# A state-space and linear-attention kernel on one core: a table factor from three products, parameter rows of 1 KB, two more table loads, and another order of the steps

## The chip, the core and the metric

The kernel runs on one core of a Trainium2 chip. The metric is the time of one execution on the device in microseconds (us). The profile shows five engines: PE (TensorE matmuls, with PEld for its weight loads), DVE (VectorE), ACT (ScalarE), POOL (GpSimd) and SP (SyncE, which issues most of the DMAs).

## The reference, cut to what matters

Both branches read the same input `x = A_u` (2048 positions, 512 channels, bf16).

```python
# branch a: S4 convolution, per channel d with N = 128 complex states
dt = exp(log_dt)[:, None];  A = A_re + 1j*A_im;  logdA = dt*A;  dB = dt*(B_re + 1j*B_im)
P = exp(logdA[:, :, None] * l)                   # l = 0 .. 2047
K = einsum("dn,dnl,dn->dl", C_re + 1j*C_im, P, dB).real
a = causal_conv(x, K) + x * Dskip                # by FFT of length 4096
# branch b: linear attention, 32 heads of 16, features softmax(+-q w_phi), softmax(+-k w_phi)
qkv = x @ wqkv;  kv = phi_k^T v;  z = sum phi_k
b = ((phi_q kv) / (phi_q z + 1e-6)) @ wo
g = sigmoid((x * gate_w).sum(-1));  out = g*a + (1-g)*b
```

The convolution kernel `K` needs the exponential of 512 x 128 complex numbers at 2048 places. The kernel builds it from factors: a place is split into a coarse step (4 values), a middle step (8 values of 64 places) and a fine step, so that a matmul over the 128 states multiplies a left table `A` (coarse times middle, with the coefficients C and dB in it) by a right table `R` (fine).

## The kernel before, in words

**Steps and order.** The program is a list of steps made by `P.add` and `P.dma` (class `Plan`), numbered as the code adds them. `Plan.ORDER` is a string with two base-64 digits for each step: it is the order in which the steps are issued, and so the order on each engine's queue. `SIDES` gives, for each step that ACT or DVE could do (most are evictions of PSUM, by `Plan.copy`, lines 175 and 177), the engine. `FOURS` has a digit for each of the 16 units of 32 channels.

**Parameters** (`prepare`). SP loads the six parameter arrays as 128 partitions by 4 pieces of 128 values (line 242, rows of 256 B), the input as `UD` in 16 DMAs with rows of 256 B (line 1465), the weights `wqk`, and constants. PE turns the parameters (line 334). From them ACT and DVE form the polar tables: `Dtab` (the middle step; magnitudes `p_d` by Exp on ACT, cosines and sines `p_sn` by Sin on ACT, the products `p_dd` and `p_de` on DVE), `Ctab` (the coarse step with coefficients; `p_ce`, `p_fc`, `p_ab`, `p_sn`, then `p_pr`, `p_px`, `p_cn` on DVE) and `Gtab`. Line 347 is the line of nearly all these products. ACT needs a table load (line 93) to go from Exp and Ln to Sin and back.

**Keys** (`keys_and_spectrum`, `attention_keys`). Once the whole input is there, PE turns it (`xT`, line 263), takes the forward FFT of the input (`psAu` to `XAu`, `psBu` to `XU`, written to DRAM as `XUd`), and for 16 blocks of 128 positions makes keys (`pk`), their exponentials on ACT (`ek`), sums on DVE (`zk`, line 662), Ln and Exp (`rz`), values (`vp`, `vb`, `vr`) and the sum `kv` (`kn`). `kvbd` closes this stage.

**Units** (`plan_conv`, `kgen`). For each of 16 units U of 32 channels: PE makes arguments, ACT takes `cs` (two Sin, in four phases of four units, each between two table loads) and `E` (Exp); DVE makes `El` (line 989), `Rh` and `Rl` (the right table, lines 1054 and 1058) and the left table in steps `A1` (line 1037), `A2` (line 1042) and, where the digit of `FOURS` is 0, `A3` (line 1047). `kps` on PE (`kgen_chunk`, line 209) multiplies left by right: 64 matmuls where `A3` has added the products up, 128 where the digit is 1 and PE adds them in PSUM. The left table has one buffer. Then `KD`, FFT stage `psA` to `XA`, `psB` to `XK`, on DVE the product `t` with the input's spectrum (line 1230), `psz` to `Zr`, a way through DRAM (`Zd`, `ZT`), `psy`, and `ou` on DVE with the gate. Beside the units the queries of four blocks run (`pq`, `eq`, `zs`, `z1` to `z5`, `em`, `ops`, `oT`). The last group, units 14 and 15, ends with `zt`, `psy32`, `ou` and the `out` DMAs (line 1341).

```python
terms = [(k, k) for k in range(2)] if not four else [(0, 0), (2, 0), (1, 1), (3, 1)]
...
c.A = g.wk.tile([128, 4, 4, 8, 32], BF16, name="A", tag="A", bufs=g.P.k["A"])   # A1 fills 0:2, A2 fills 2:4
nc.vector.tensor_tensor(out=c.A[:, 0:2], in0=c.A[:, 0:2], in1=c.A[:, 2:4], op=ALU.add)   # A3
```

## Time and profile before

| what | value |
|---|---|
| three runs | 253.78, 251.02, 252.83 us; median 252.83 us |
| the profiled execution | 252.17 us, of which the profile's span is 250.4 us |
| granted TensorE clock, mean | 0.944 |
| busy share of the span | DVE 90%, ACT 84%, PE 81%, PEld 57%, POOL 1% |
| DMA | 38.23 MB in 61922 packets, mean 153 GB/s |
| chain that ended last | PE 28%, DVE 24%, ACT 23%, DMA 10%, SP's queue 7%, issue 5% |

How to read it: busy time of an engine is the union of its instructions. DVE and ACT instructions that follow one another overlap by about 0.1 us, so a stage's time is nearer to the distance of their starts than to the sum of their durations. [...] Idle time of an engine costs only where that engine sets the pace.

### The profile page before, as it was taken

What the parts mean: (1) busy time and instruction counts of PE and PEld (TensorE: products, weight loads), DVE (VectorE), ACT (ScalarE), POOL (GpSimd) and SP (SyncE); (2) the same over time, 40 slices, a digit from 0 to 9 for tenths busy, and PEclk for the clock granted to TensorE, in tenths of its full rate; (3) what the DMA queues carried; (4) which work ended last, traced back from release to release, by engine and by line L of the source; (5) the groups of instructions that cost most, each with busy time, mean ns of one, the idle gap of its engine ahead of it and who ended that gap; (6) DMA issues with size and microseconds to landing.
All of it is one profiled execution on the core that took longest, in us unless ns stands there. A gap on an engine that the chain in (4) does not pass through costs nothing.

```text
span 250.4 us, 9850 instructions
## 1 busy us (share of the span) xinstructions
PE 202.3 (81%) x4412; PEld 141.8 (57%) x4437; DVE 224.2 (90%) x287; ACT 211.0 (84%) x291; POOL 2.4 (1%) x7
## 2 busy tenths in 40 slices
PE   0695999999956468798797778889999789998970
PEld 0584755447734434256456646765777576877550
DVE  0388999989899988999999999999999999999680
ACT  2058999999999999999999999999999999974430
POOL 0200000000000000000000000000000000000000
PEclk9999999999995569999979999999999999999985
DMA  6999910236280477400619129804896879998664
GB/s 134 275 174 159 404 49 4 90 105 134 56 256 0 145 235 223 160 3 13 174 49 240 38 73 243 265 3 92 197 209 192 219 206 234 225 235 165 185 171 75
DMA packets 61922, 38.23 MB, mean 153 GB/s; under 512 B 40632, under 2 KB 57272, under 8 KB 61496
## 3 DMA queue, kind: packets, MB, share of 16 engines
q1 hardware_dynamic: 61880, 37.61, 60.0%
q8 instruction: 34, 0.56, 1.0%
q14 instruction: 8, 0.07, 0.1%
HBM read 24.49 MB, written 13.11 MB: 150 GB/s over the span
## 4 chain that ended last, share of the span: by engine, by line
PE 28%; DVE 24%; ACT 23%; DMA 10%; SPq 7%; issue 5%; ACTq 0%; DVEq 0%
ACT Eq L96 4%; PE pk L635 4%; ACT cs L96 4%; DMA UD<-in_A_u_dram 4%; PE vp L683 4%; SPq L1465 3%; ACT E L96 3%; PE kps L209 2%; DMA ZT<-Zd 2%; PE psB L542 2%; ACT XA L175 2%; ACT L93 2%; DVE t L1230 2%; PE psy L750 2%; PE psz L1256 2%
## 5 line engine op out<-in xcount | busy, mean ns | idle before, releaser
L209 PEld LDWEIGHTS <-A 128*32 128x32 bf16 x1664 | 28.5, 160 | 6.2 <-issue 3.6
L209 PE MATMUL kps<-R,A 128*32 128x64 bf16 x1664 | 30.3, 229 | 1.8 <-DVE A L1042 0.5
L96 ACT ACTIVATE cs<-args 128x1024 bf16<-128x1024 f32 x32 | 30.7, 1050 | 0.2 <-PE args L953 0.2
L1058 DVE TENSOR_TENSOR R<-E,cs 128x2048 bf16<-128x2048 bf16 x16 | 19.5, 1217 | 0.0
L1037 DVE TENSOR_TENSOR A<-Ctab,Dtab 128x2048 bf16<-128x2048 bf16 x16 | 19.5, 1217 | 0.0
L1054 DVE TENSOR_TENSOR R<-E,cs 128x2048 bf16<-128x2048 bf16 x16 | 19.5, 1217 | 0.0
L1042 DVE TENSOR_TENSOR A<-Ctab,Dtab 128x2048 bf16<-128x2048 bf16 x16 | 19.5, 1217 | 0.0
L175 ACT CAST Zr<-psz 128x1024 bf16<-128x1024 f32 (+1 forms) x17 | 16.5, 974 | 2.5 <-issue 1.2
L542 PE MATMUL psB<-XAu,TB 64*128 64x128 bf16 x256 | 12.8, 262 | 7.1 <-ACT xst L175 4.9
L175 ACT CAST XK<-psB 128x1024 bf16<-128x1024 f32 (+1 forms) x15 | 15.0, 1010 | 3.8 <-PE psB L222 2.3
L175 ACT CAST XA<-psA 128x1024 bf16<-128x1024 f32 (+1 forms) x16 | 15.6, 1002 | 3.2 <-PE psA L216 3.2
L683 PE MATMUL vp<-WW,xT 128*128 128x512 bf16 x59 | 16.9, 403 | 0.8 <-issue 0.7
L1230 DVE TENSOR_TENSOR t<-XUX,XK 128x2048 bf16<-128x2048 bf16 x14 | 17.0, 1218 | 0.5 <-ACT XK L175 0.5
L96 ACT ACTIVATE Ek<-pk 128x512 bf16<-128x512 f32 x32 | 16.8, 602 | 0.4 <-PE pk L635 0.2
L769 PE MATMUL pq<-xT,Wqp 128*128 128x512 bf16 x64 | 16.5, 396 | 0.6 <-ACT Eq L96 0.6
L96 ACT ACTIVATE Eq<-pq 128x512 bf16<-128x512 f32 (+1 forms) x28 | 16.7, 711 | 0.2 <-PE pq L769 0.2
L96 ACT ACTIVATE E<-args 128x1024 bf16<-128x1024 f32 x16 | 16.8, 1058 | 0.0
L542 PEld LDWEIGHTS <-TB 64*128 64x128 bf16 x256 | 10.3, 116 | 11.2 <-issue 11.0
L1256 PE MATMUL psz<-t,small 128*128 128x512 bf16 x49 | 14.6, 380 | 2.0 <-ACT cs L96 0.5
L635 PE MATMUL pk<-WW,xT 128*128 128x512 bf16 x57 | 15.5, 380 | 0.5 <-issue 0.2
L662 DVE TENSOR_REDUCE Zk<-Ek 128x64 f32<-128x1024 bf16 x12 | 14.0, 1209 | 0.0
L222 PE MATMUL psB<-XA,TB 128*128 128x128 bf16 (+2 forms) x160 | 9.6, 205 | 4.1 <-ACT XA L175 1.4
(178 smaller groups left out, 463.8 us busy)
## 6 DMA issues: line engine op xcount, KB each, us to landing
XUX<-XUd SPq DMA_DIRECT2D x24, 256.0 KB, 4.2
XUd<-xst SPq DMA_DIRECT2D x8, 512.0 KB, 3.1
ax<-apd SPq DMA_DIRECT2D x16, 256.0 KB, 4.9
Zd<-Zr SPq DMA_DIRECT2D x14, 256.0 KB, 4.5
ZT<-Zd SPq DMA_DIRECT2D x12, 256.0 KB, 5.7
UD<-in_A_u_dram SPq DMA_DIRECT2D x16, 128.0 KB, 4.8
XUd<-xst SPq DMA_DIRECT2D x8, 256.0 KB, 3.9
XUX<-XUd SPq DMA_DIRECT2D x4, 512.0 KB, 6.2
```

Of the source, the lines that this page charges most:

```text
L96: return self.nc.scalar.activation(**kw)
L175: self.nc.scalar.copy(out=o, in_=i)
L209: nc.tensor.matmul(kps[32 * dj:32 * dj + 32, g4, e, :], lhsT=A[:, ka, :, :, d].rearrange("p a b -> p (a b)"), rhs=R[:, kr, d, :], start=(i ...
L542: nc.tensor.matmul(box.ps[:, c2, sl, :], lhsT=fc.TB[rows, b0:b0 + 2].rearrange("p a b -> p (a b)"), rhs=X.t[rows, k, r0 + sl].rearrange("p ...
L635: nc.tensor.matmul(box.ps[:], lhsT=xT[:, st, kt, :], rhs=g.WW[:, kt, :], start=(kt == 0), stop=(kt == 3))
L683: nc.tensor.matmul(box.ps[:], lhsT=xT[:, st, kt, :], rhs=g.WW[:, 4 + kt, :], start=(kt == 0), stop=(kt == 3))
L1037: nc.vector.tensor_tensor(out=c.A[:, 0:2].rearrange("p o a b c -> p (o a) b c"), in0=g.C[U // 8][:, 0:2, :, d0 % 256:d0 % 256 + 32].rearra ...
L1042: nc.vector.tensor_tensor(out=c.A[:, 2:4].rearrange("p o a b c -> p (o a) b c"), in0=g.C[U // 8][:, 1:3, :, d0 % 256:d0 % 256 + 32].rearra ...
L1054: nc.vector.tensor_tensor(out=c.R[:, :, :, 32:64], in0=t.E[:, 1].unsqueeze(1).to_broadcast([128, 2, 32, 32]), in1=t.cs[:], op=ALU.mult)
L1058: nc.vector.tensor_tensor(out=c.R[:, :, :, 0:32], in0=t.E[:, 0].unsqueeze(1).to_broadcast([128, 2, 32, 32]), in1=t.cs[:, ::-1, :, ::-1], o ...
L1230: nc.vector.tensor_tensor(out=box.t, in0=Ls[r0 // ns].X[:], in1=box.XK[:].unsqueeze(1).to_broadcast([128, 2, 1024]), op=ALU.mult)
L1256: nc.tensor.matmul(box.ps[:, hb, :], lhsT=fc.TI[:, k].rearrange("p h a t -> p (h a t)"), rhs=box.t[:, k, 512 * hb:512 * hb + 512], start=( ...
```

## The change

1. **Left table from three products.** With the complex factors C and D, the two sums that PE needs are formed from three products, not four. `Ctab` holds for each half of the channels the real part and the sum and difference of imaginary and real part; `Dtab` holds real part, imaginary part and their difference (`DS0`, `DS1`). Each unit has one DVE instruction `A1` over 3 x 4 x 8 x 32 values instead of `A1`, `A2` and, for six units, `A3`; `kps` has four terms, 128 matmuls, for all units. `FOURS` goes.
2. **Parameters in rows of 1 KB.** Channel 4p+g is on partition p, not 128g+p; one row of a DMA has four channels. PE writes the turned parameters with a stride of 4. `log_dt` by partition has its own small DMA (`ldc`) instead of a place among the turned rows. The identity matrix has a DMA of its own (`kid`). The statistics `pz` are written in 1 KB rows as well.
3. **Table loads.** The Sin part of the parameters stands between two loads of its own (`tabT`, and a new `tabL`), and the first phase of `cs` has its own `tabT`: 11 loads for 9.
4. **Buffers.** `vb` lies in the third plane of `Dtab` with four buffers for two; the gate's row `zrow` lies in blocks of `TB` that are free by then.
5. **Order.** `ORDER`, `SIDES` and `RINGS` are all new. The `out` DMAs of the end are in part on ACT's queue.

```diff
-            terms = [(k, k) for k in range(2)] if not four else [(0, 0), (2, 0), (1, 1), (3, 1)]
+    terms = ((2, 0), (2, 1), (1, 0), (0, 1)) if h == 0 else ((0, 0), (0, 1), (2, 0), (1, 1))
...
-        P.dma("par", 0.45, 2.5, lambda k=k, src=src: nc.sync.dma_start(out=g.rawd[k][:], in_=src.rearrange("(g p) n -> p g n", p=128)),
+        P.dma("par", 0.45, 2.5, lambda k=k, src=src: nc.sync.dma_start(out=g.rawd[k][:], in_=src.rearrange("(p g) n -> p g n", p=128)),
...
-        V("p_px", lambda h=h: tt(C[h][:, 0:2], F.P[:], F.Q[:], ALU.add), r="t0 t1 t5 t6", w=f"Cn{h} Ci{h}")
-        V("p_cn", lambda h=h: nc.vector.tensor_scalar(out=C[h][:, 2], in0=C[h][:, 0], scalar1=-1.0, scalar2=None, op0=ALU.mult), r=f"Cn{h}", w=f"C{h}")
+        V("p_cr", lambda h=h, oR=oR: tt(C[h][:, oR], F.P[:, 0], F.Q[:, 0], ALU.add), r="t0 t1 t5 t6", w=f"Cn{h} Ci{h} C{h}")
+        V("p_ci", lambda: tt(F.P[:, 1], F.P[:, 1], F.Q[:, 1], ALU.add), r="t0 t1", w="t5 t6")
+        V("p_cm", lambda h=h, oM=oM, oR=oR: tt(C[h][:, oM], F.P[:, 1], C[h][:, oR], ALU.subtract), r="t5 t6", w=f"C{h} Ci{h} Cn{h}")
+        V("p_cp", lambda h=h, oP=oP, oR=oR: tt(C[h][:, oP], F.P[:, 1], C[h][:, oR], ALU.add), r="t5 t6", w=f"C{h} Ci{h} Cn{h}")
...
+    g.tabL = P.add("ACT", "tabL", lambda: act.begin(LN_EXP), [n for n in P.nodes if n.name == "p_sn"], sets="L", tab="T")
...
+    P.add("DVE", "DS0", lambda: nc.vector.tensor_tensor(out=g.D[:, 2], in0=g.D[:, 0], in1=g.D[:, 1], op=ALU.subtract), vs + [polar], rw=("", "DS"))
...
-    prev = []
+    prev = [g.tabL]
...
-        b = P.add("ACT", "tabT", lambda: act.begin(TRIG), [ra[0][0]] + prev, sets="T", tab="L") if prev else polar
+        b = P.add("ACT", "tabT", lambda: act.begin(TRIG), prev, sets="T", tab="L")
...
+                c.A = g.wk.tile([128, 3, 4, 8, 32], BF16, name="A", tag="A", bufs=g.P.k["A"])
+                h, c0 = U // 8, d0 % 256
+                nc.vector.tensor_tensor(out=c.A[:], in0=g.C[h][:, :, :, c0:c0 + 32].unsqueeze(3).to_broadcast([128, 3, 4, 8, 32]),
+                                        in1=g.D[:, 2 * h:2 * h + 3, U % 8].unsqueeze(2).to_broadcast([128, 3, 4, 8, 32]), op=ALU.mult)
```

## The prediction

> **What bounds the kernel now.** I read the page first, then a table of busy times by stage, then the groups of instructions, and last the order of time around the stages' ends.

> ```profile
> span 250.4 us, 9850 instructions
> PE   0695999999956468798797778889999789998970
> DVE  0388999989899988999999999999999999999680
> ACT  2058999999999999999999999999999999974430
> DMA  6999910236280477400619129804896879998664
> PE 28%; DVE 24%; ACT 23%; DMA 10%; SPq 7%; issue 5%; ACTq 0%; DVEq 0%
> ```

> Three stretches are to be seen; the last row, the chain's shares, names no single engine. For 25 us the engines are half empty and DMA is full. Then DVE and ACT are both full to about 223 us. The last 27 us are a chain with holes. The ends of these stretches are the first eviction `XAu` on ACT (all input is there), the first `E` of the units and, for the last unit, the last `E`:

> ```profile
> 24.77 1.05 PE L263 MATMUL xps<-small,UD 128*128 128x128 bf16 x16 [1.85 <-DMA UD<-in_A_u_dram]
> 26.86 1.01 ACT L175 CAST XAu<-psA 128x1024 bf16<-128x1024 f32 x1
> 93.72 7.50 ACT L96 ACTIVATE cs<-args 128x1024 bf16<-128x1024 f32 x8
> 101.23 1.28 ACT L93 ACT_TABLE_LOAD   x1
> 102.53 1.02 ACT L96 ACTIVATE E<-args 128x1024 bf16<-128x1024 f32 x1
> 216.85 1.08 ACT L96 ACTIVATE E<-args 128x1024 bf16<-128x1024 f32 x1
> 243.80 0.42 DVE L1330 TENSOR_TENSOR xT<-psy,gT 128x256 bf16<-128x256 f32 x1 [0.50 <-PE psy L1319]
> ```

> The busy times of the stages between such marks (columns: PE, PEld, DVE, ACT, POOL, clock, DMA share, GB/s):

> ```profile
> 0.00:26.86 26.86, 14.85 (x162) 13.38 (x164) 14.69 (x27) 11.99 (x14) 2.41 (x7) 1.00 1.09 199
> 26.86:102.53 75.67, 63.34 (x1058) 38.55 (x1067) 71.99 (x111) 72.56 (x115) 0.00 (x0) 0.89 0.46 139
> 102.53:160.00 57.47, 47.69 (x1247) 32.92 (x1247) 56.82 (x64) 57.09 (x83) 0.00 (x0) 0.97 0.43 117
> 160.00:223.00 63.00, 58.01 (x1456) 44.37 (x1463) 62.72 (x64) 60.18 (x69) 0.00 (x0) 1.00 0.72 181
> 223.00:250.40 27.40, 18.41 (x511) 12.60 (x508) 17.94 (x25) 9.21 (x14) 0.00 (x0) 0.86 0.69 154
> ```

> From 102.53 to 223 us DVE is busy for 119.5 of 120.5 us and ACT for 117.3: both set the pace, and a gain on one alone is worth nothing. PE has 105.7 us, 88%, but 92% in the second part.

> **The change part by part.** Durations:

> ```profile
> L1037 DVE TENSOR_TENSOR A<-Ctab,Dtab 128x2048 bf16<-128x2048 bf16 x16 | 19.5, 1217 | 0.0
> L1042 DVE TENSOR_TENSOR A<-Ctab,Dtab 128x2048 bf16<-128x2048 bf16 x16 | 19.5, 1217 | 0.0
> L1047 DVE TENSOR_TENSOR A<-A 128x2048 bf16<-128x2048 bf16 x6 | 7.3, 1217 | 0.0
> L347 DVE TENSOR_TENSOR Dtab<-Dtab,trg 128x1024 bf16<-128x1024 bf16 x8 | 5.3, 688 | 0.8 <-ACT trg L96 0.6
> L347 DVE TENSOR_TENSOR Ctab<-ppx,ppy 128x2048 bf16<-128x2048 bf16 x2 | 2.4, 1222 | 0.0
> L393 DVE TENSOR_SCALAR Ctab<-Ctab 128x1024 bf16<-128x1024 bf16 x2 | 0.8, 420 | 0.0
> L177 DVE CAST XAu<-psA 128x1024 bf16<-128x1024 f32 x7 | 8.3, 1215 | 0.2 <-PE psA L517 0.2
> L175 ACT CAST XA<-psA 128x1024 bf16<-128x1024 f32 x15 | 15.0, 1029 | 0.3 <-PE psA L216 0.3
> L96 ACT ACTIVATE Dtab<-pt 128x512 bf16<-128x512 f32 x8 | 5.1, 633 | 0.0
> L93 ACT ACT_TABLE_LOAD x9 | 11.5, 1283 | 0.9 <-PEq L1576 0.7
> 200.46 2.22 PE L209 MATMUL kps<-R,A 128*32 128x64 bf16 x128 [0.29 <-ACT XK L175]
> 210.06 1.21 PE L209 MATMUL kps<-R,A 128*32 128x64 bf16 x64
> ```

> *Left table.* Removed: 38 instructions of 1.217 us, 46.3 us of DVE. Added: 16 of 3072 values, which the trace doesn't show. From 1024 to 2048 values a product of this kind grows by 1.217 - 0.688 = 0.53 us, so 3072 take 1.75 us, 28.0 us in all. The bounds are 1.7 us and, at the rate of an eviction from PSUM (1.215 us for 1024), 3.6 us. I take 1.75: `A1` already reads both operands in broadcast and in runs of 32, and needs no longer than the plain product of 2048 at line 347 (1.222). `DS0` and `DS1` cost 2 x 1.22, and the new `Ctab` products 2 x (4 x 0.688 - 1.222 - 0.420) = 2.2. DVE's net is -13.7 us. The same edit gives PE 6 x 64 matmuls more: the step from 64 to 128 is 2.22 - 1.21 = 1.0 us, for units 0, 8, 10, 13, 14 and 15. The left table still has one buffer, so the next `A1` waits for `kps`; in the rows above this wait is 0.0.

> *Evictions.* Written out against the numbered steps, the side digits move 3 `XA`, 2 `XK`, 2 `Zr`, a `Y`, a `Zrh`, 2 `xT` and a `udc` to DVE, and 2 `XAu`, 1 `XU`, 2 `bs3`, a `wTe` and three halves of the last unit to ACT: +4.5 us for DVE, -4.9 us for ACT (1.215 against 1.03 us for 1024 values). DVE falls by 9 us of 224, ACT, with the loads, by 2 of 211.

> Now by stage, from both order strings. On a full ACT one instruction costs the distance of starts: 7.50 / 8 = 0.94 us for a `cs` of 1.05, so 0.92 for an eviction and 0.53 for a `p_d`.

> *Head (to the first `XAu`).* The queue of SP now has four of the six parameter arrays, constants, `wqk`, `ldc`, `kid`, `wsm` and `ld` ahead of the first piece of input. What counts is the last piece, since every `XAu` needs all.

> ```profile
> 6.00:9.00 3.00, 1.99 (x17) 1.73 (x17) 0.89 (x3) 0.00 (x0) 0.00 (x0) 1.00 0.99 346
> 15.00:18.00 3.00, 2.88 (x30) 2.64 (x29) 2.93 (x7) 2.25 (x3) 0.00 (x0) 1.00 1.43 171
> 10.11 5.17 SPq L1465 DMA_DIRECT2D UD<-in_A_u_dram  x8
> ```

> DMA is full there: with 256 B rows it moves 171 GB/s, and 346 where `wqk` with its 2 KB rows comes in. The parameters (0.79 MB) would take 2.3 us, not 4.6. Against that SP issues one DMA more, 0.65 us at the input's rate (5.17 for eight), if the queue were the limit. Bounds: -2.3 to +0.7. ACT also gets 2.7 us more work ahead of this mark (5 `p_d`, `p_ab`, `wTe`, less 2 `xT`), DVE about as much; their 15 and 12 us of idle time cover it, if the parameters are early. As the turning of all the input now falls into the last third of the head, I take **-1.5**.

> *First `XAu` to first `E`.* ACT sets the pace (72.6 of 75.7 us). Added: 2 loads (2.6), 2 `XAu` and 1 `XU` (2.8). Gone: 5 `p_d`, `p_ab`, `udc` (-4.6). **+0.8**. DVE has 2.5 us less with `kvbd` put aside, which moves behind the first `A1`. The second load is a wait for ACT's queue: the last two `rz` and `g_e` stand behind it, and `vr`, `kn`, `DS0`, and so `A1`, wait for them. In the rows above, a load is just the gap between two neighbours: 101.23 + 1.28, then `E` at 102.53, 1.30 us in all. [...]

> *First to last `E`.* ACT loses 5 `XA`, 3 `Zr`, a `KD` and an `XK` and gets a `bs3`: -8.7 us. DVE: `A` -15.8, evictions +5, `DS1` +1.1, `kvbd` and `g_c` from before +2.6, an `ou` and two `t64` pushed behind: -9. So both could end 8.7 us sooner. PE is then the question: five of its six longer units lie here (+5.0), about as much goes behind the last unit (`psy128`, `pya`, `psz`, `opsL`), so some 106 us stay in a stage that would be 111.8 us, 95%. At the 92% that PE reaches from 160 us on, 106 us need 115.4, a gain of 5; at 88%, none. I take **-6.5**, between 92% and 95%, with bounds of 0 and -8.7.

> *Tail.* Moved behind the last `E`: 3.9 us for ACT, 4.1 for DVE, 4.9 for PE. The holes of the last stage (9 us on DVE and PE, 18 on ACT) cover part of it, and the last unit's own chain loses 1.7 us, as one instruction replaces three. Bounds -1.7 and +4.9; I take the middle, **+1.6**. The output ends on a queue:

> ```profile
> 242.50 5.35 SPq L1341 DMA_DIRECT2D out_dram<-xT  x8
> ```

> The last four of these wait for the last `ou`. Afterwards ACT issues the last six and SP two, at 0.67 us each as on SP; the first two of ACT's six can start before the last `ou`, so I count nothing, with +1.3 as the end if they can't.

> The sum is -1.5 + 0.8 - 6.5 + 1.6 = -5.6: a span of 244.8 us. The profiled execution took 252.17 us, 1.77 beyond its span, so **246.6 us**. The median of the runs, 252.83, lies 0.7 above that execution. About 1%, 2.5 us, is what can be told from no change.

> **The rivals.**
> 1. *All of the gain on DVE and ACT comes through*: -8.7 in the units, -2.3 in the head, +0.8, tail +0.8: 242.8, and 240 if the tail ends at its lower bound. For it: DVE and ACT are at 97 to 99% already. Against: PE at 95%.
> 2. *PE takes over as the bound.* The units' stage stays at 88 to 90% PE: 0 to -2.7, so 250.4 to 253.1. For it: PE's share of the chain (28%) is already the largest. Against: 92% is shown from 160 us on.
> 3. *Slower.* The place is the block of sines between the two loads. It is a dialogue: DVE fills, ACT takes the sine into single buffers, DVE multiplies. DVE has 3.0 us more in it, ACT 2.6. If the two add rather than overlap, everything up to `kvbd` and the first `A1` comes 5.6 us later; from there on it decides the sign if the units give less than 3. Time: 252.2 - 1.5 + 5.6 + 1.6 - 2 = 255.9. For it: ACT already has a gap there, for a transfer:

> ```profile
> 88.20 1.93 ACT L175 CAST xst<-psB 128x1024 bf16<-128x1024 f32 x2 [0.87 <-DMA XUd<-xst]
> ```

> Against: eleven `XAu`, `XU` and `vb` stand in ACT's order between the sines, and fill the waits.
> [...]
> 5. *The change doesn't do what it says*: the 3072-value product runs at 3.6 us, +30 us of DVE, some 273 us.

> **How the numbers follow.** Forecast 0.58 (243.5 to 249.7), rival 1 0.13, rival 4 0.03: faster by over 1%, 0.74. Rival 2 is the no-change case, 0.15. Rivals 3 and 5, 0.09 and 0.02: slower, 0.11. The range goes from 241.0, most of rival 1, to 253.5, all of rival 2; some 0.16 is left out.

> **What would show it.** Line `A1`: 16 instructions at 1.75 us. `kps`: 2048 matmuls, still no DVE idle time ahead of `A1`. 11 loads at 1.28 us with no gap behind. The last `xps` near 22.5, the first `XAu` near 25.4, the first `E` near 101.8, the last near 209.6, the last `ou` near 238. I am wrong if the first `E` is later than 104 (block of sines), if PE stays below 90% between the marks while DVE and ACT go idle (PE or its latencies as the bound), or if more than 35 us follow the last `E`.

## The result and the profile after

The changed kernel is slower: 261.75 us (median of 4 runs, 260.49 to 262.72) against 252.96 us (251.02 to 253.78) for the kernel before in the same session, a ratio of 1.0356 with an interval of 1.0283 to 1.043. The profiled execution took 261.78 us, with a span of 260.0 us, against 252.17 us and 250.4 us. The forecast was 246.6 us. Ratios, here and below, leave disturbed runs out, which medians do not, so the two can differ a little.

The rows of the page that answer to those of before:

```profile
span 260.0 us, 10608 instructions
PE   0677999999764268998787979889897989689950
DVE  0699988998999998999999999999579999437850
PEclk9999999999999559999999999999799999799985
DMA  7899720457407465018240587479246989494716
q8 instruction: 37, 0.61, 1.0%
PE 44%; ACT 33%; issue 6%; DVE 6%; DMA 6%; SPq 1%; ACTq 0%
```

PE's share of the chain has gone from 28% to 44%, DVE's from 24% to 6%. DVE has holes (the digits 5 and 7) where before it was full to slice 37. PEclk has single slices of 7 from slice 29 on; before there was none so late. The row of q8 comes back below. The groups of instructions:

```profile
L1052 DVE TENSOR_TENSOR A<-Ctab,Dtab 128x3072 bf16<-128x3072 bf16 x16 | 28.0, 1751 | 1.8 <-PE kps L207 1.7
L207 PE MATMUL kps<-R,A 128*32 128x64 bf16 x2048 | 36.2, 228 | 3.3 <-issue 2.4
```

`A1` costs 1.751 us, as forecast. `kps` has 2.4 us of idle time whose releaser is "issue": PE waited for nothing that the profile shows. Now the stages, cut at the first `XAu`, the first `E`, 160 us, the first matmul of unit 15's `kps` and the last matmul (columns as in the prediction); first the changed kernel, then the last three rows of the kernel before in the same cut:

```profile
0.00:26.60 26.60, 14.33 (x160) 13.22 (x161) 17.41 (x32) 14.77 (x19) 2.94 (x7) 1.00 1.01 210
26.60:101.38 74.78, 59.69 (x1062) 36.69 (x1071) 70.69 (x106) 72.96 (x112) 0.00 (x0) 0.91 0.45 136
101.38:160.00 58.62, 50.52 (x1410) 37.51 (x1414) 56.58 (x64) 57.62 (x85) 0.00 (x0) 1.00 0.42 114
160.00:229.95 69.95, 61.38 (x1648) 46.66 (x1648) 60.93 (x57) 55.76 (x62) 0.00 (x0) 0.95 0.70 173
229.95:250.80 20.85, 19.07 (x539) 13.39 (x540) 12.95 (x17) 8.35 (x14) 0.00 (x0) 1.00 0.57 130
250.80:260.00 9.20, 0.00 (x0) 0.00 (x0) 1.23 (x1) 0.00 (x0) 0.00 (x0) 0.56 0.55 111
```

```profile
160.00:228.95 68.95, 63.39 (x1611) 48.69 (x1617) 68.27 (x69) 63.53 (x73) 0.00 (x0) 1.00 0.74 179
228.95:243.70 14.75, 12.99 (x349) 8.28 (x344) 11.96 (x18) 5.86 (x10) 0.00 (x0) 0.97 0.71 187
243.70:250.40 6.70, 0.04 (x4) 0.00 (x0) 0.42 (x1) 0.00 (x0) 0.00 (x0) 0.50 0.47 78
```

Up to the first `E` the change is ahead by 1.1 us, and at unit 15's `kps` behind by 1.0, although between 160 us and that mark DVE has 7.3 us and ACT 7.8 us less to do. Behind that mark it loses 6.1 us more to the last matmul, and 2.5 us from there to the end.

Where PE stood still shows in the timeline of PE (in brackets the idle time before the row, and its releaser):

```profile
169.95 0.27 PE L220 MATMUL psB<-XA,TB 128*128 128x128 bf16 x2 [0.73 <-issue]
180.23 1.15 PE L207 MATMUL kps<-R,A 128*32 128x64 bf16 x58
182.88 1.33 PE L207 MATMUL kps<-R,A 128*32 128x64 bf16 x70 [1.50 <-issue]
213.15 0.32 PE L207 MATMUL kps<-R,A 128*32 128x64 bf16 x7 [0.90 <-issue]
223.72 0.51 PE L1326 MATMUL psy<-ZT,TJ 64*32 64x128 bf16 x23 [2.26 <-issue]
234.35 0.24 PE L220 MATMUL psB<-XA,TB 128*128 128x32 bf16 x3 [1.30 <-issue]
```

These are 6.7 us. All lie inside a group whose operands had long been there: a `kps` of 128 matmuls breaks after 58. The row of q8 on the page points at the cause: its kind is "instruction", and its 37 transfers in the trace have 16384 bytes each. This queue's rows in the kernel before and in few_wide304 (an experiment below):

```profile
q8 instruction: 34, 0.56, 1.0%
q8 instruction: 29, 0.48, 0.8%
```

The kernel before has 768 instructions of PE fewer than the change and 3 blocks fewer (34 for 37), few_wide304 has 2048 fewer and 8 blocks fewer (29): 256 for each block. By this count PE's program comes in over this queue. Counted over PE's instructions (a matmul and its weight load are two), the stops are 256 or a multiple of it apart (to within the few records that this trace lacks), and each ends 1.2 to 1.6 us after a block of q8 has landed (at 168.74, 181.39, 211.72, 222.09 and 233.00). A `kps` of 128 matmuls is, by the same count, one whole block and lasts 2.2 us.

These are four stretches from PE's entry into a block to the start of the next block's transfer; the share of DMA is the last but one column:

```profile
107.46:108.26 0.80, 0.80 (x58) 0.80 (x55) 0.80 (x1) 0.80 (x2) 0.00 (x0) 1.00 0.00 0
125.63:126.34 0.71, 0.71 (x59) 0.71 (x52) 0.71 (x2) 0.71 (x2) 0.00 (x0) 1.00 0.00 0
176.35:180.01 3.66, 3.65 (x83) 2.26 (x78) 3.59 (x4) 3.53 (x5) 0.00 (x0) 1.00 1.03 218
219.11:221.19 2.08, 2.08 (x132) 2.04 (x136) 2.08 (x3) 0.98 (x1) 0.00 (x0) 1.00 0.96 246
```

At a DMA share of 0.00 the transfer started 0.71 and 0.80 us after the entry, at 0.96 and 1.03 it was 2.08 and 3.66 us. The 37 transfers of this trace took 0.88 to 1.69 us, and PE went on 1.21 to 1.63 us after the landing at the five stops. From entry to going on that adds up to an estimate of about 3 us with DMA free, and to 6.5 us in the longest case (3.66 + 1.35 + 1.49, the stop at 182.88). By this estimate a block that PE issues faster than that is followed by a stop.

Behind the two longest stops the granted clock (third number from the right) falls:

```profile
180.20:183.60 3.40, 1.90 (x109) 1.76 (x107) 2.69 (x3) 2.88 (x4) 0.00 (x0) 1.00 0.90 218
183.60:187.00 3.40, 3.40 (x89) 2.12 (x83) 1.76 (x1) 1.34 (x2) 0.00 (x0) 0.50 0.07 23
221.20:224.60 3.40, 1.14 (x48) 0.86 (x48) 2.01 (x2) 0.59 (x1) 0.00 (x0) 0.99 0.10 34
224.60:228.00 3.40, 3.40 (x47) 3.23 (x41) 1.04 (x1) 1.93 (x2) 0.00 (x0) 0.51 0.86 200
```

PE is busy for all of the 3.4 us behind each, at a clock of 0.50 and 0.51: an estimate of 1.7 us lost in each, if it does half the work in them.

The trace of the kernel before has two such stops, much shorter ones, at the same place of a block:

```profile
193.57 1.24 PE L209 MATMUL kps<-R,A 128*32 128x64 bf16 x66 [0.17 <-issue]
228.15 0.34 PE L222 MATMUL psB<-XA,TB 128*128 128x32 bf16 x7 [0.52 <-issue]
```

### The profile page after: what moved, and what is told of

Its sections match the earlier page's. It is cut to its first block, busy times and chain, and to the rows that moved or that the text cites. A ratio compares the mean times of both kernels' runs of the same rounds, so it can differ in the third digit from the quotient of the medians.

```text
span 260.0 us, 10608 instructions
## 1 busy us (share of the span) xinstructions
PE 205.0 (79%) x4800; PEld 147.5 (57%) x4821; DVE 219.8 (85%) x274; ACT 209.5 (81%) x290; POOL 2.9 (1%) x7
## 4 chain that ended last, share of the span: by engine, by line
PE 44%; ACT 33%; issue 6%; DVE 6%; DMA 6%; SPq 1%; ACTq 0%
PE kps L207 9%; ACT cs L96 7%; PE pk L644 4%; ACT L93 4%; PE vp L692 4%; PE pq L783 4%; PE psy L764 3%; DMA vecs<-in_A_log_dt_dram 2%; ACT E L96 2%; PE psy L1326 2%; ACT Zr L173 2%; PE psB L220 2%; ACT trg L96 2%; PE psz L1263 2%; DMA XUd<-xst 2%
## 5 line engine op out<-in xcount | busy, mean ns | idle before, releaser
L207 PE MATMUL kps<-R,A 128*32 128x64 bf16 x2048 | 36.2, 228 | 3.3 <-issue 2.4
L207 PEld LDWEIGHTS <-A 128*32 128x32 bf16 x2048 | 34.5, 161 | 7.1 <-issue 3.9
L96 ACT ACTIVATE cs<-args 128x1024 bf16<-128x1024 f32 x32 | 30.8, 1051 | 0.0
L1052 DVE TENSOR_TENSOR A<-Ctab,Dtab 128x3072 bf16<-128x3072 bf16 x16 | 28.0, 1751 | 1.8 <-PE kps L207 1.7
L1061 DVE TENSOR_TENSOR R<-E,cs 128x2048 bf16<-128x2048 bf16 x16 | 19.5, 1217 | 0.9 <-ACT E L96 0.9
L1237 DVE TENSOR_TENSOR t<-XUX,XK 128x2048 bf16<-128x2048 bf16 x14 | 16.8, 1217 | 3.8 <-ACT XK L173 3.8
L96 ACT ACTIVATE E<-args 128x1024 bf16<-128x1024 f32 x16 | 16.7, 1048 | 3.0 <-issue 1.8
L173 ACT CAST XK<-psB 128x1024 bf16<-128x1024 f32 (+1 forms) x14 | 13.3, 983 | 6.5 <-PE psB L220 4.8
L173 ACT CAST Zr<-psz 128x1024 bf16<-128x1024 f32 (+1 forms) x14 | 13.8, 990 | 5.4 <-PE psz L1263 3.0
L96 ACT ACTIVATE Eq<-pq 128x512 bf16<-128x512 f32 (+1 forms) x28 | 16.7, 694 | 0.3 <-PE pq L783 0.2
L96 ACT ACTIVATE Ek<-pk 128x512 bf16<-128x512 f32 x32 | 16.6, 617 | 0.2 <-PE pk L644 0.2
L692 PE MATMUL vp<-WW,xT 128*128 128x512 bf16 x59 | 15.2, 379 | 0.3 <-issue 0.2
L551 PE MATMUL psB<-XAu,TB 64*128 64x128 bf16 x256 | 9.3, 222 | 7.7 <-ACT xst L173 5.6
L93 ACT ACT_TABLE_LOAD x11 | 14.1, 1283 | 0.9 <-PEq L1588 0.7
L551 PEld LDWEIGHTS <-TB 64*128 64x128 bf16 x256 | 7.8, 96 | 10.2 <-issue 8.3
L968 PE MATMUL args<-selE,statC 64*128 64x512 bf16 x32 | 7.1, 434 | 7.2 <-ACT cs L96 3.3
L173 ACT CAST XA<-psA 128x1024 bf16<-128x1024 f32 (+1 forms) x13 | 12.5, 990 | 0.4 <-PE psA L214 0.3
```

What stands on the lines that cost most here:

```text
L93: return self.nc.scalar.preload_act_table_set(name)
L96: return self.nc.scalar.activation(**kw)
L173: self.nc.scalar.copy(out=o, in_=i)
L207: nc.tensor.matmul(kps[32 * dj:32 * dj + 32, g4, e, :], lhsT=A[:, ka, :, :, d].rearrange("p a b -> p (a b)"), rhs=R[:, kr, d, :], start=(i ...
L551: nc.tensor.matmul(box.ps[:, c2, sl, :], lhsT=fc.TB[rows, b0:b0 + 2].rearrange("p a b -> p (a b)"), rhs=X.t[rows, k, r0 + sl].rearrange("p ...
L692: nc.tensor.matmul(box.ps[:], lhsT=xT[:, st, kt, :], rhs=g.WW[:, 4 + kt, :], start=(kt == 0), stop=(kt == 3))
```

## The experiments

Three theories stood at the start. F: PE runs out of instructions. W: PE has 384 matmuls more to do, and is the bound. O: the new order costs the time. A fourth, Q, came with the tail: the division of the output between two queues.

**Fewer instructions, PE's time taken down, then put back.**

```diff
-    terms = ((2, 0), (2, 1), (1, 0), (0, 1)) if h == 0 else ((0, 0), (0, 1), (2, 0), (1, 1))
+    terms = ((2, 0), (2, 1)) if h == 0 else ((0, 0), (0, 1))
-  rhs=R[:, kr, d, :]                 # 128 matmuls of 64 columns
+  rhs=wide[:, r:r + 192]             # 64 matmuls of 192 (few_instr), 256, 304 columns
```

> The changed kernel with kps as 64 matmuls of 192 columns in place of 128 of 64 columns, for all units: two of the four terms are left out and the columns are three times as wide, so the values are not those of the reference. PE's time for a kps should stay within half a us of the 2.2 us, but PE has 2048 instructions fewer (7596 for 9644). Theory F: the stops and the two drops of the clock after them go, some 7 to 9 us: 253 to 255 us. Theories O and W: within 1.5 us of 261.8, apart from what kps itself gets shorter or longer by (to be read from its own duration).

> As few_instr, but with 256 columns a matmul instead of 192: 64 matmuls in every kps, two of the four terms left out, so the values are not those of the reference. At 192 columns a kps took 1.57 us, 24.5 ns a matmul, so that 256 columns should bring it back to 2.1 us, near the 2.2 us of the changed kernel, with 2048 instructions of PE fewer. Theory F (PE's instructions arrive too late): the gain of few_instr stays, 250.5 to 254 us. Theory W (PE's time for the matmuls themselves): the gain goes, 258 to 261 us. Theory O (order): it goes too, and few_instr has gained by its shorter kps alone.

> As few_wide256, with 304 columns a matmul (two of the four terms left out, so the values are not those of the reference). A kps took 2.01 us from its first to its last matmul in the changed kernel, 1.31 at 192 columns and 1.71 at 256, so 304 columns should give 2.0: the same time of PE as in the changed kernel in half the instructions of kps. Theory F (PE's instructions arrive too late): 250.5 to 254 us, as at 256 columns. Theory W (PE's time for the matmuls): 258 to 262 us.

| kernel | a `kps`, first to last matmul | median us | ratio to before, interval |
|---|---|---|---|
| the change | 2.01 us, 128 matmuls | 261.75 | 1.0356 (1.0283 to 1.043) |
| few_instr | 1.31 us, 64 | 250.56 | 0.9977 (0.9937 to 1.0017) |
| few_wide256 | 1.71 us, 64 | 251.13 | 0.9956 (0.9906 to 1.0005) |
| few_wide304 | 2.00 us, 64 | 252.05 | 1.002 (0.9988 to 1.0053) |

From 192 to 304 columns PE gets 16 x 0.7 = 11 us more to do, and the time rises by 1.5 us. At the `kps` of the change in half the instructions few_wide304 is 3.4% faster than the change. W falls for the new order: PE's time is nearly free here, its instructions are not. (Half the matmuls are also half the weight loads, and wider columns; these runs do not tell the three apart.) Rows of few_wide304, the page and the timeline of PE, then the stages from 160 us on:

```profile
L210 PE MATMUL kps<-R,A 128*32 128x304 bf16 x1024 | 36.8, 296 | 0.8 <-ACT XA L173 0.5
226.16 0.24 PE L223 MATMUL psB<-XA,TB 128*128 128x32 bf16 x3 [0.93 <-issue]
```

```profile
160.00:222.10 62.10, 58.82 (x1168) 43.53 (x1160) 60.22 (x57) 55.54 (x62) 0.00 (x0) 1.00 0.76 190
222.10:242.60 20.50, 19.21 (x477) 13.22 (x476) 13.32 (x18) 8.35 (x14) 0.00 (x0) 1.00 0.62 143
242.60:251.80 9.20, 0.00 (x0) 0.00 (x0) 1.22 (x1) 0.00 (x0) 0.00 (x0) 0.68 0.55 111
```

`kps` keeps PE as busy as in the change (36.8 against 36.2 us), "issue" is gone from its row, one stop is left, and the clock stays at 1.00. From 160 us to unit 15's `kps` it takes 62.1 us where the change took 69.95. The last two stages are those of the change, to 0.4 us.

**The same in the last six units only.**

```diff
-  kgen_chunk(nc, K.ps[:, cc], c.A, c.R, U // 8)
+  (kgen_wide if U >= 10 else kgen_chunk)(nc, K.ps[:, cc], c.A, c.R, U // 8)   # 304 columns from unit 10 on
```

> The changed kernel with the 64 wide matmuls of few_wide304 in the last six units only (10 to 15; their values are not those of the reference). Theory F with the stops of the trace: four of the five stops and both drops of the clock lie from unit 10 on, so nearly all of the gain stays: 252 to 255.5 us. If all units share the loss alike: 258 us.

253.62 us, ratio 1.0076 (1.0045 to 1.0108): some 2.8 of the 3.4% come from the last six units, where four of the five stops and both drops of the clock were.

**The instructions alone, in the old kernel.**

```diff
-    FOURS = ("0111111101011000")
+    FOURS = ("1111111111111111")      # before_fours1
```

> The kernel before with the digit 1 in FOURS for all 16 units: DVE loses six sums of 1.22 us (7.3 us), PE gets 6 x 64 matmuls more, as in the change; order and tables stay. Theory O: the same as before or faster by up to 3 us (250 to 253), since PE has room in the old order. Theory W: slower by up to 6 us (255 to 259). Theory F: stops of PE appear at one place modulo 256 instructions, 2 to 4 us more of them than the 1 to 2 us of before: 252 to 256 us.

```diff
-  terms = [(k, k) for k in range(2)] if not four else ...    # 64 or 128 matmuls of 64 columns
+  terms = ((0, 0), (1, 1))                                   # before_wide256: 64 of 256 columns, all units
```

> The kernel before with every kps as 64 matmuls of 256 columns (values not those of the reference): the six units with the digit 0 go from 1.2 to about 2.1 us of PE, as in the change, the ten others stay near 2.2 us; DVE keeps its sums A3. PE's work is that of before with all digits 1 (266.7 us), at 2048 instructions fewer. Theory F: 250 to 254 us. Theory W: 258 to 266 us, DVE waiting for kps ahead of A1 as there (4.5 us).

before_fours1: 266.75 us, ratio 1.0606 (1.0505 to 1.0707), more than any of the theories gave; before_wide256: 255.3 us, 1.0128 (1.0035 to 1.0221). DVE has 7.3 us less to do in the first, and it is the slower of the two. Its groups:

```profile
L209 PE MATMUL kps<-R,A 128*32 128x64 bf16 x2048 | 37.2, 230 | 5.4 <-issue 3.2 <-DVE R L1058 1.4 <-DVE A L1042 0.5
L1037 DVE TENSOR_TENSOR A<-Ctab,Dtab 128x2048 bf16<-128x2048 bf16 x16 | 19.5, 1220 | 4.5 <-PE kps L209 4.5
L175 ACT CAST KD<-kps 128x1024 bf16<-128x1024 f32 (+1 forms) x8 | 7.8, 970 | 6.3 <-PE kps L209 6.3
```

PE stops (3.2 us in `kps`, some 8 us in all, from the distances of its instructions at the block boundaries; the change has 7.7 by that measure). DVE waits for it, since the left table has one buffer, and ACT, which evicts `kps`. before_wide256 has no such stop, and is slower than the kernel before by 1.3%. But its `kps` takes 1.71 us in every unit: 0.7 more than before in the six units, 0.3 less in the ten others, so 1.3 us more in all, where before_fours1 has 6. So PE's time was not held equal here, and how much of the loss W has in the old order stays open.

**The change without its order.**

```diff
-    ORDER, SIDES, RINGS = those of the change
+    ORDER, SIDES, RINGS = those of the kernel before, the new steps at their places; the two new table loads left out
```

> All of the change but the order: the left table from three products, 128 matmuls in every kps, the 1 KB rows, the new buffers, with the steps in the order, on the engines and in the rings of the kernel before; the two new table loads are left out too, since the old order needs none there. Theory O: the old order keeps its tail of 33.5 us after the last E, and the saved DVE time comes on top: 246 to 250 us. Theory F: the old order gets 768 more instructions of PE and stops as well, 2 to 5 us of them: 250 to 257 us. Theory W: 6 units with 1 us more of PE each, 252 to 258 us.

266.68 us, ratio 1.0493 (1.0421 to 1.0565). O falls as the whole cause: the old order is no better with the new `kps`. Its 3072-value product waits for `kps` as in before_fours1:

```profile
L1034 DVE TENSOR_TENSOR A<-Ctab,Dtab 128x3072 bf16<-128x3072 bf16 x16 | 28.1, 1755 | 5.4 <-PE kps L189 5.2
```

**The place of the block boundaries.**

```diff
+  nc.gpsimd.memset(dz[:], 0.0)
+  for i in range(96):                # ahead of PE's first real instruction
+      nc.tensor.matmul(dps[i % 2][0:32, :], lhsT=dz[:], rhs=dz[:, 0:8], start=True, stop=True, ...)
```

> The changed kernel with 96 tiny matmuls (192 instructions of TensorE) put in front of the first real one, in the 8 us in which PE waits for its first data; nothing else differs. Theory F (PE's program arrives in blocks of 256 instructions, and PE runs out of it inside dense groups): the five stops at place 175 to 180 of a block (169.2, 181.4, 212.2, 221.4, 233.0 us; 6.7 us in all) move to other instructions, again at one place of the block counted with the 192. The three late ones (4.5 us) should shrink to about 1 us, and new ones of about 1 us each appear near 108, 122, 142, 156 and 183 us, where DVE and ACT set the pace: 256 to 260 us. Theory O (the new order of the last units costs the time) and theory W (PE simply has 384 matmuls more to do): nothing moves, 261.8 within 1 us.

259.29 us, ratio 1.0286 (1.0213 to 1.0359). The stops moved to other groups, all at the old place counted with the 192:

```profile
109.11 0.29 PE L807 MATMUL zs<-Eq,SSw 128*32 128x128 bf16 x8 [0.56 <-issue]
123.47 0.26 PE L207 MATMUL kps<-R,A 128*32 128x64 bf16 x4 [0.22 <-issue]
144.37 0.49 PE L220 MATMUL psB<-XA,TB 128*128 128x128 bf16 x6 [0.22 <-issue]
184.59 0.83 PE L207 MATMUL kps<-R,A 128*32 128x64 bf16 x38 [1.51 <-issue]
```

The new ones near 108, 122 and 142 us were forecast, and those at 212 and 233 us are gone. But the one forecast near 156 did not come, and the late ones did not shrink as expected: 1.51 us at 184.59 and 2.00 us at 224.71 (inside `psA`), each with 3.4 us at a clock of 0.50 behind it, as in the change. The gain of 0.7% lies within the two intervals, so only the place is shown by this run, not the time.

**Products summed on DVE, so that `kps` has 64 matmuls and leaves no term out.**

```diff
+  if U in SUMMED:                    # the common product is added to the two others, 2048 values
+      lo, x = (0, 2) if h == 0 else (1, 0)
+      nc.vector.tensor_tensor(out=c.A[:, lo:lo + 2], in0=c.A[:, lo:lo + 2], in1=c.A[:, x:x + 1].to_broadcast([128, 2, 4, 8, 32]), op=ALU.add)
```

> The changed kernel, but for units 0, 8, 10, 13, 14 and 15, the six that had 64 matmuls before, DVE adds the common product to the two others (one sum of 2048 values, 1.22 us, 7.3 us in all), and kps has 64 matmuls again. PE is back at the work and the instructions of before, order and all else stay those of the change. Theories F and W: the lost time comes back, 248 to 254 us. Theory O: no gain, and the sums cost, 262 to 266 us.

> The sums for six units of sum6 (256.3 us) and the out steps on SP together. By theories F and Q, 253.5 to 255.5 us; without Q, 256 us.

> As sum6_sp, with the sums for units 9, 11 and 12 too, so that all from 8 on have 64 matmuls: 3 x 128 instructions of PE fewer and 3 x 1.22 us of DVE more. Theory F: in sum6 PE still stops inside the kps of units 10 and 12 (1.2 and 1.6 us longer than their like); these stops go, and DVE's 3.7 us are hidden in part: 251 to 254 us. If the late units are bound by DVE: 255 to 258 us.

> The same sums for the same six units with the order, sides and rings of the kernel before. PE's work and instructions are those of before; DVE has 6.4 us less than before (13.7 less 7.3). Theories F and W: no more than before and up to 4 us less, 247 to 252 us, since ACT, with unchanged work, is as full as DVE. Theory O says nothing else here, but by it this kernel is faster than the same sums in the new order by 8 us or more.

> The old order with the left table from three products and the sum of 1.22 us on DVE in all 16 units, 64 matmuls in every kps. Against the kernel before: PE 1280 instructions and some 10 us fewer, DVE about 2 us more, all results right. Theory F: PE had 1 to 2 us of stops there, and its latency goes: 249 to 253 us. If DVE and ACT alone set the pace in the old order: 253 to 256 us.

| kernel | units with the sum | median us | ratio to before, interval |
|---|---|---|---|
| sum6 | 6, new order | 256.25 | 1.0186 (1.0105 to 1.0268) |
| sum6_sp | 6, new order, output on SP | 257.5 | 1.0201 (1.0119 to 1.0283) |
| sum9_sp | 9, new order, output on SP | 257.76 | 1.0215 (1.0152 to 1.0278) |
| oldorder_sum6 | 6, old order | 254.38 | 1.0131 (1.0059 to 1.0202) |
| oldorder_sum16 | 16, old order | 262.75 | 1.0436 (1.0381 to 1.0491) |

sum6 gives back half of the loss, and PE still stops inside the `kps` of units 10 and 12 (its timeline, first fence). Taking more instructions from PE by work on DVE does not help further. oldorder_sum16, with 2048 instructions of PE fewer than the change, is slower than the kernel before by 4%: its left table takes 47.7 us of DVE (its groups, second fence), DVE is busy for 231.5 us instead of 224.2, and the rest of its 11 us is not explained. sum6_sp, sum9_sp and both kernels in the old order came out above what F gave them: F alone does not account for their times.

```profile
183.26 0.31 PE L212 MATMUL kps<-R,A 128*32 128x64 bf16 x6 [0.99 <-issue]
205.05 0.31 PE L212 MATMUL kps<-R,A 128*32 128x64 bf16 x7 [1.35 <-issue]
```

```profile
L1039 DVE TENSOR_TENSOR A<-Ctab,Dtab 128x3072 bf16<-128x3072 bf16 x16 | 28.1, 1754 | 0.7 <-PE kps L194 0.5
L1043 DVE TENSOR_TENSOR A<-A 128x2048 bf16<-128x2048 bf16 x16 | 19.6, 1225 | 0.6
```

oldorder_sum6 shows something else: DVE is busy for 220.0 us instead of 224.2, with as many instructions of PE as in the kernel before, and the time is not lower. Why is open. None of these beats the kernel before.

**The output's queues.**

```diff
-  SIDES: the last three out steps on ACT
+  SIDES: the last three out steps on SP
```

> The changed kernel with the last three out steps issued by SP instead of ACT, as before; nothing else differs. In the changed kernel SP's fourth out waits 8.0 us for an out of ACT, since both use one DMA semaphore, and the six DMAs behind it leave up to 256.8 us. Theory Q (the division between the two queues costs about 2 us of the tail): 259 to 260.5 us. If it costs nothing: 261.8 within 0.7 us.

> few_wide304 (252.1 us, values not those of the reference) with the last three out steps on SP instead of ACT. Without PE's stops the tail can be compared: from the last matmul to the end of the span few_wide256 took 9.4 us, as the changed kernel did, the kernel before 6.9. Theory Q: SP's fourth out no longer waits for one of ACT, and the end comes 1.5 to 2.5 us sooner: 249.5 to 250.6 us. Otherwise 252 within 0.7.

outs_sp: 259.87 us, 1.0343 (1.0255 to 1.0431), no difference that can be told. Its stops are others again, 9.9 us of them by the distance of the instructions, where the change has 7.7: counted over all of PE's records in its trace, they are at 5825, 6337, 6849, 7873, 8129, 8385 and 8897, all 193 beyond a multiple of 256. few304_sp, with the wide matmuls: 251.29 us, 0.9986 (0.9957 to 1.0016) against 1.002; from the last matmul to the end 8.6 us for 9.2. So Q is worth 0.6 us in these traces, less than expected, and the ratios do not tell it from nothing. Another 0.8 of the 2.5 us of that stage is the last `ou`, which has 1024 values here (the row below) and 256 before (0.42 us, in the prediction); the rest stays open.

```profile
250.86 1.23 DVE L1337 TENSOR_TENSOR xT<-psy,gT 128x1024 bf16<-128x1024 f32 x1 [0.75 <-PE psy L1326]
```

**The converse of few_wide304, which failed as a test.**

```diff
+  for _ in range(2):
+      nc.tensor.ldweights(A[:, ka, :, :, d].rearrange("p a b -> p (a b)"), tile_position=(0, 32 * dj))
   nc.tensor.matmul(...)              # as in few_wide304
```

> few_wide304 (252.1 us; two of the four terms left out, values not those of the reference) with two more load-weight instructions of the same weights ahead of each matmul of kps: 256 instructions in every kps again, as in the changed kernel, and no matmul more. Theory F: PE stops at the block boundaries again, and the time goes back to 258 to 264 us, at a kps of about 2 us where it doesn't stop. If the width of the matmuls was what helped: 252 us within 1.5, apart from what each kps gets longer by (to be read from it).

312.1 us, ratio 1.2387 (1.2312 to 1.2462). A `kps` took 4.89 us for 2.00, so the added weight loads were not hidden; PE no longer issued 256 instructions in less than the estimate of 3 us, and no stop is in the trace. It says nothing on F, and that instructions alone, at an equal `kps`, bring the loss back was not shown in this way.

## Why the prediction was wrong, step by step

| step | forecast us | the change | few_wide304 |
|---|---|---|---|
| head, to the first `XAu` | -1.5 | -0.3 | -1.3 |
| first `XAu` to first `E` | +0.8 | -0.9 | -0.2 |
| first `E` to unit 15's `kps` | -6.5 (to the last `E`) | +2.2 | -5.4 |
| from there to the last matmul | | +6.1 | +5.8 |
| last matmul to the end | +1.6 with the row above | +2.5 | +2.5 |
| sum | -5.6 | +9.6 | +1.4 |

The differences are those of the stage rows above and of the kernel before (26.86, 75.67, 126.42, 14.75 and 6.70 us), and for few_wide304 of its marks at 25.60, 101.10, 222.10, 242.60 and 251.80. The mark is unit 15's `kps` and not the last `E` of the forecast: in the new order that `E` comes early (it is the second of this row and starts at 211.15, forecast 209.6), 18.8 us ahead of the `kps` that uses it, 12.1 us before.

```profile
210.23 1.94 ACT L96 ACTIVATE E<-args 128x1024 bf16<-128x1024 f32 x2 [0.48 <-PE args L990]
```

Measured to the last `E`, the units' term would read -4.5 for -6.5, and the tail +15.3 for +1.6 (-7.5 and +10.3 in few_wide304): a mark that comes early hands the loss to the next stage.

- **Head, loads, left table.** `A1` at 1.751 us held, with 11 loads of 1.28 us, no dialogue in the block of sines (rival 3) and no 3072-value product at 3.6 us (rival 5). The 0.03 for rival 4 stands for a price of a table load beyond its own length, and no run shows one: ACT's next instruction came 0.01 us behind each load but the first. The first `E` at 101.38 for 101.8 is in part luck: the head gained 1.2 us less than forecast (few_wide304, with the same head, 0.2 less), and the next stage cost 1.7 less. DVE's busy time fell by 4.4 us (224.2 to 219.8 on the pages), not by 9.
- **First `E` to unit 15's `kps`, the term that failed first.** The forecast's working was "about 106 us of PE in a stage that would be 111.8", and each longer `kps` at 1.0 us. Without the stops the term comes out nearly as forecast (-5.4). What it lacked is that a `kps` of 128 matmuls is a whole block of instructions, issued (2.01 us) faster than the next one arrives (about 3 to 6.5 us by the estimate above). Four of the five stops (5.4 us) and the two drops of the clock (3.4 us, an estimate) lie ahead of the mark, 8.8 us, and the change reaches it 7.6 us later than few_wide304 does, counted from the first `E`. Two short stops, 0.17 and 0.52 us, were in the trace of before, and I read over them. Of the three signs that the prediction set for itself, two came, PE below 90% while DVE and ACT go idle (61.38 of 69.95 us, 88%) and more than 35 us behind the last `E` (48.85). That is rival 2's condition, but its mechanism, PE's work, was shown wrong by few_wide304.
- **The tail, mis-sized.** Forecast +1.6, measured +8.6, with or without stops (+8.3 in few_wide304). I let "the holes of the last stage (9 us on DVE and PE)" cover part of 4.9 us that moved behind the last unit. 6.7 us of those 9 lie behind the last matmul, where only DMA runs, and no work of PE fits in. The true holes of PE were 14.75 - 12.99 = 1.8 us, and PE's busy time there grew by 6.1 us (12.99 to 19.07), as much as that stage did.
- **Output.** "I count nothing, with +1.3 as the end" was 2.5 us; 0.6 of it is the division between the queues, 0.8 the longer last `ou`.

So with only one short stop left the change would have been no faster than the kernel before (1.002): what the units gain, the tail gives back, and what lies in the tail is set by the new order. That follows from few_wide304, which leaves out two of the four terms; a version of the change with fewer instructions, all four terms and no more work on DVE wasn't found.

## What to carry to other kernels

Count instructions of PE, not only its microseconds: in this kernel a dense run of 256 (128 small matmuls with their weight loads) took 2.01 us, less than a block took to arrive, by the estimate above about 3 us with DMA idle and up to 6.5 us beside a burst. "issue" as the releaser in the middle of a matmul group, at distances of a multiple of 256, was the sign. When a saving on one engine is paid with small matmuls, price them by the block. Count holes as room for moved work only up to the last instruction of the engine that is to fill them.

## What the runs showed of the hardware that I had not expected

```profile
232.78 0.24 PE L220 MATMUL psB<-XA,TB 128*128 128x32 bf16 x3 [2.99 <-issue]
231.13:234.54 3.41, 1.76 (x35) 1.01 (x39) 1.22 (x1) 0.61 (x1) 0.00 (x0) 1.00 0.17 26
234.54:237.95 3.41, 3.41 (x122) 3.08 (x115) 2.70 (x4) 1.77 (x4) 0.00 (x0) 1.00 0.57 94
```

- With four column tiles, 128 matmuls of 64 columns take 2.01 us and 64 of 304 columns 2.00 us: 8192 columns in all in the time of 19456, so at 64 columns something other than the number of columns sets the time of `kps`; what does is not shown. Two more weight loads for each of 64 matmuls added 2.9 us (4.89 for 2.00), 23 ns each.
